# Q projection and O normalisation packed two head groups to a tile, with a new tile table

## The chip, the core and the metric

The kernel runs on one core of one Trainium2 chip. The metric is the device time of one execution in microseconds. Several executions are timed; all that are quoted here are of the state "fast". The span in a profile is some 1.7 to 2.0 us shorter than the time of the same execution. The experiments were made on four chips, each time beside the kernel before, whose median there was 802.84 to 803.36 us; times of different runs are compared across chips with that spread in mind.

## The reference, cut to what matters

```python
B, S, D, H = 1, 2048, 512, 32;  Dh = 16
xn = layernorm(x)
q = (xn @ wq) in 32 heads;  k = xn @ wk;  v = xn @ wv        # one k and v for all heads
p = softmax(q k^T / sqrt(Dh))                                # 32 heads x 2048 x 2048
attn = (p v, heads side by side) @ wo
ffn  = gelu(xn @ w1 + b1) @ w2 + b2                          # F = 1792
return x + attn + ffn
```

The dearest thing is the exponential of 32 x 2048 x 2048 scores. A head has only 16 columns, so everything that is laid out by head fills few of the 128 rows of a tile unless something packs it.

## The kernel before

Queries are cut into 4 blocks of 512 and heads into 8 groups of 4. A score tile is 128 keys x 512 queries of one head; there are 2048 of them, handled in 683 units of three. Each of the four heads of a group sits at its own 32-row strip (16 rows of Q, one row for the softmax shift, 15 of zeros), so that TensorE can work on three tiles at once: near 300 us in the profile before, three score matmuls together take 0.39 us, as long as one.

```python
def scores(u):                       # TensorE: three tiles into three PSUM banks, two sets of banks
    for o, l, rh, q0 in pieces:
        ins = e.matmul(o, l, rh, start=True, stop=True, tile_position=(q0, 0))
def exp(u):                          # ScalarE: the two or three tiles that are not VectorE's
    exps.append(act(lambda e: e.activation(E[:, s0:s0 + na, :], bank(b0, na)..., ACT.Exp, scale=LN2 / 128.0), ...))
    for i, t in enumerate(ts):
        if is_d[t]:
            p1(t, 3 * x + i)         # VectorE: PSUM to int16, then four shifted copies a batch of three
```

A string DTAB has one character a unit and says which tile VectorE takes: "." none, "0" or "2" the first or last. Such a tile costs TensorE five value matmuls (one a shifted copy) in place of one.

Beside this stream run the feed-forward part, the output projection and the Q projection, all as side work in the gaps. Q and O before the change:

```python
def q_proj(tb, hq, bk, ...):         # weights padded to 32 columns a head: 4 heads fill 128 columns
    for d in range(DT):
        (f or mm)(bank(bk), wqp[:, d, 4 * hq:4 * hq + 4, :]..., xnT[:, d, tb * TBW:(tb + 1) * TBW], ...)
def q_evac(tb, hq, bk, **kw):
    dve(lambda e: e.tensor_copy(QT[:, hq, :], bank(bk)), ...)            # cast, one group
    dve(lambda e: e.tensor_tensor(sqq[:, sq(hq), :], QT[:, hq, :], QT[:, hq, :], ALU.mult), ...)
def o_evac(gg):                      # ... reciprocal row sums through DRAM into rbc ...
    onorm[gg] = dve(lambda e: e.tensor_tensor(oT[:, gg % NOT, :], Of[:, i, :], rbc[:, i, :], ALU.mult), ...)
    for j in range(HG):              # then 4 small copies pack 16 rows each
        dma("sp", oTp[r0:r0 + Dh, ...], oT[32 * j:32 * j + Dh, ...], ...)
```

The order in which each engine runs its instructions is fixed when the program is built: a list scheduler (`Prog.schedule`) with estimated durations sorts all operations. Its computed end of the last operation is called **the scheduler's clock** below. It is no measurement.

Of the kernel before, what the change touches and what calls it, by code (L numbers as in the profile page):

```python
# [7 lines left out]
ALU = mybir.AluOpType  # L8
# [30 lines left out]
NE_ND_KB = (24, 8, 3)  # L39
# [11 lines left out]
DTAB = "...00.0020..2.0202....00022022..2002.0.0...000...0.02.02.2220...2022.20222.220.202...200.00.00.20.000.20..20.02.0.22000.02000...202.22.002.0.00.20....220..00022002.2.20...0002.02022.0.2220....222222.22.22020.00...22222.22.00.2.000.0..220...2.0220..0202....22202.020.2.22.222...202..0...2.02200.2...22.0.2..2..00..2000...22.0022.00.2002.02...20220.02.2202.2020...2222.20.202202.2220...2022.200220..0.00....222.0..2022.20.0.20....200.02.20.0..0200....2.220..220.200.02....222.20...02000.200..2.000..0222222.020....2202.22002022..022...2222.02.020222.2.20..222200.0202.222.22.....2..20.2.202.2..0.......0...2202..220.20..2.0..20.0..2.200000...0200.2.2200.00202....22022200..020.2000...."  # L51
# [5 lines left out]
S_LAT = 0.27  # L57
YS = 9
# [367 lines left out]
def bass_parallel_sum__grouped_kv_mqa__dense_activation_gelu__prompt_kernel(  # L426
# [27 lines left out]
    NOT, NPR, NSQ = 3, 5, 4  # L454
# [6 lines left out]
    with ExitStack() as es:  # L461
# [6 lines left out]
        wq_s = ub[:, 8:12, :]  # L468
# [3 lines left out]
        wqp = sb([P, DT, H, 32], bf, "wqp")  # L472
# [19 lines left out]
        sel8 = sb([P, 8, 32], bf, "sel8")  # L492
        selr = sb([P, 4, 32], bf, "selr")
        sel8R = sb([P, 8, 32], bf, "sel8R")
# [21 lines left out]
        hb = sb([P, 6 + NSQ, TBW], bf, "hb")  # L516
# [6 lines left out]
        rbc = sb([P, 2, TBW], f32, "rbc")  # L523
        rX = rbc[:, 1, :].rearrange("p (i r) -> p i r", i=4)
        rd_dram = nc.dram_tensor("rden_rows", [NTB * NGR, HG * TBW], f32).ap()
        oT = sb([P, NOT, TBW], bf, "oT")
# [51 lines left out]
        dma("act", wq_s, A_wq.rearrange("(k p) n -> p k n", p=P), "d_wq", w=[("u", i) for i in range(8, 12)], due=0.0,  # L578
# [22 lines left out]
        dve(lambda e: e.memset(wqp[:, :, :, Dh:32], 0.0), w=["wqp"], n=1024, due=0.1)  # L601
# [4 lines left out]
        sel_diag = bass.AP(sel8[:].tensor, sel8[:].offset, [list(sel8[:].ap[0]), [33, 8], [8, 4]])  # L606
# [6 lines left out]
        for v, c in enumerate((1.0,) + SPL_C):  # L613
            setup(lambda e, v=v, c=c: e.memset(V1[:, v, :, Dh:Dh + 1], c), r=["V1"], w=["V1"], due=11.0)
        setup(lambda e: e.memset(sel8[:], 0.0), w=["sel8"], occ=0.3, due=12.0)
        setup(lambda e: e.tensor_copy(sel_diag, mask4[:].unsqueeze(1).to_broadcast([P, 8, 4])),
              r=["mask4", "sel8"], w=["sel8"], due=12.0)
# [114 lines left out]
        def q_proj(tb, hq, bk, f=None, **kw):  # L732
            for d in range(DT):
                (f or mm)(bank(bk), wqp[:, d, 4 * hq:4 * hq + 4, :].rearrange("p a n -> p (a n)"),
                          xnT[:, d, tb * TBW:(tb + 1) * TBW], d == 0, d == DT - 1,
                          r=["wqp" if hq else "wqp0"] + tr(4 * tb, 4 * tb + 4), w=[B(bk)], **kw)

        def sq(hq):
            return 6 + hq % NSQ

        def q_evac(tb, hq, bk, **kw):
            dve(lambda e: e.tensor_copy(QT[:, hq, :], bank(bk)),  # L742
                w=[B(bk)] + [(B(bk), j) for j in range(4)] + [("QT", hq)] + [("QTm", hq, j) for j in range(4)], **kw)
            dve(lambda e: e.tensor_tensor(sqq[:, sq(hq), :], QT[:, hq, :], QT[:, hq, :], ALU.mult),
                r=[("QT", hq)], w=[("h", sq(hq))], mode=2, **kw)

        def q_first(hq, bk):
            q_proj(0, hq, bk, due=10.5)
            q_evac(0, hq, bk, due=Q_DUE)

        def q_first_m(hq, bk):
            mm(bank(bk), selr[:].rearrange("p a n -> p (a n)"), sqq[:, sq(hq), :], False, True,
               r=["selr", ("h", sq(hq))], w=[B(bk)], skip=True, due=16.0)
            dve(lambda e: e.tensor_scalar(QT[:, hq, :].bitcast(i16), bank(bk).bitcast(i32), isc[:, 0:1], ibi[:, 0:1],
                                          ALU.mult, ALU.add),
                r=["isc", "ibi"], w=[B(bk), ("QT", hq)] + [("QTm", hq, j) for j in range(4)], due=16.0)
# [7 lines left out]
        def wq_first():  # L764
            setup(lambda e: e.tensor_copy(wqp[:, :, 0:4, 0:Dh], wq_s[:, :, 0:64].rearrange("p k (h n) -> p k h n", n=Dh)),
                  r=[("u", i) for i in range(8, 12)] + ["wqp"], w=["wqp0"], occ=0.45, due=9.0)
# [6 lines left out]
        for _, _, kind, a in sorted(steps, key=lambda s: s[:2]):  # L773
            if kind == "ln":
                ln_batch(list(range(*a[:2])), a[2])
            elif kind == "tr":
                x_T(list(range(*a[0])), a[1], a[2])
            elif kind == "k":
                k_proj(list(range(*a[0])), a[1])
            elif kind == "v":  # L780
                v_tiles(range(*a))
                if a[1] in (NVA, NT):
                    k_max(0 if a[1] == NVA else NVA, a[1], land(a[1] - 1) + KM_DUE)
            else:
                wq_first()
                q_first(0, 7)
# [9 lines left out]
        q_first_m(0, 7)  # L796
# [8 lines left out]
        for v, c in enumerate(SPL_C):  # L805
# [3 lines left out]
        setup(lambda e: e.tensor_copy(wqp[:, :, 4:H, 0:Dh], wq_s[:, :, 64:D].rearrange("p k (h n) -> p k h n", n=Dh)),  # L809
              r=[("u", i) for i in range(8, 12)] + ["wqp"], w=["wqp"], occ=2.7, due=19.0, after=[pr.writer["ibi"]])  # L810
# [24 lines left out]
        def scores(u):  # L835
# [3 lines left out]
            for i, t in enumerate(ts):  # L839
# [4 lines left out]
                r += [("KT", kt), ("QT", g), ("QTm", g, j)]  # L844
# [65 lines left out]
        def o_evac(gg):  # L910
# [7 lines left out]
            for j in range(HG):  # L918
                src = rd_dram[gg:gg + 1, j * TBW:(j + 1) * TBW]
                dma("sp", rbc[32 * j:32 * j + 32, i, :], bass.AP(src.tensor, src.offset, [[0, 32], [1, TBW]]),  # L920
                    f"d_rb{i}{j}", r=[("rd", i)], w=[("rbc", i, j)])
            tb, g = divmod(gg, NGR)
            onorm[gg] = dve(lambda e: e.tensor_tensor(oT[:, gg % NOT, :], Of[:, i, :], rbc[:, i, :], ALU.mult),  # L923
                            r=[("Of", i)] + [("rbc", i, j) for j in range(HG)], w=[("oT", gg % NOT)], allow=3.0)
            pp, h = divmod(gg, 2)
            if gg == NTB * NGR - 2:
                setup(lambda e: e.memset(oTp[64:P, pp % NPR, :], 0.0), w=[("oTp", pp % NPR, 1, j) for j in range(HG)], occ=0.4)
            for j in range(HG):
                r0 = 64 * h + Dh * j
                dma("sp", oTp[r0:r0 + Dh, pp % NPR, :], oT[32 * j:32 * j + Dh, gg % NOT, :], f"d_op{gg % NOT}{j}",  # L930
                    r=[("oT", gg % NOT)], w=[("oTp", pp % NPR, h, j)])

        def o_norm_last(gg):
            RB1 = [("rbc", 1, j) for j in range(HG)]
            for h in range(2):
                c = slice(h * 256, h * 256 + 256)
                dve(lambda e, c=c: e.tensor_copy(Of[:, 0, c], pO[:, c]), w=["O", ("Of", 2 * h)], n=256, due=0.0)
            for h in range(2):
                for i in (2 * h, 2 * h + 1):
                    mm(bank(h)[:, 4 * i:4 * i + 4], Of[:, 0, i * P:(i + 1) * P], selL[:], True, True,  # L940
                       r=[("Of", 2 * h), "selL"], w=[B(h)], occ=0.2, due=0.0)
            for h in range(2):
# [5 lines left out]
                if h == 0:  # L948
                    dve(lambda e, o=o, i_=i_: e.tensor_copy(o, i_), r=[("rT", h)], w=[("rX", h)] + RB1, n=256, due=0.0)
                else:  # L950
                    act(lambda e, o=o, i_=i_: e.activation(o, i_, ACT.Copy), r=[("rT", h)], w=[("rX", h)] + RB1, n=256, due=0.0)
# [4 lines left out]
            for h in range(2):  # L956
                c = slice(h * 256, h * 256 + 256)
                dve(lambda e, h=h, c=c: e.tensor_tensor(oT[:, gg % NOT, c], Of[:, 0, c], bank(h)[:, 128:384], ALU.mult),
                    r=[("Of", 2 * h)], w=[B(h), ("oT", gg % NOT) if h == 0 else ("oTl", 1)], n=256, due=0.0)

        def q_group(tb, hqs, rel):
            for hq in hqs:
                q_proj(tb, hq, 7, mm4, allow=QP_ALLOW)
                q_evac(tb, hq, 7, allow=EV_ALLOW)

        def q_m(tb, hqs, **rel):
            pq = tb % 2
            for n, hq in enumerate(hqs):
                mm(pM[0:32, :], sel8R[:, hq, :], sqq[:, sq(hq), :], n == 0, n == len(hqs) - 1, r=["sel8R", ("h", sq(hq))], w=[M4[0]], tp=(0, 0), kind="side", tag=(None, 0))
# [4 lines left out]
            for j in range(4):  # L974
                dst = QT[32 * j + 16:32 * j + 17, h0:h0 + n, :]
                dma("sp", dst, mT[8 * j + h0:8 * j + h0 + n, :], f"d_m{j}",
                    r=["mT"] + [("QT", hq) for hq in hqs], w=[("QTm", hq, j) for hq in hqs])
# [28 lines left out]
        def wo_mm(tb, i, ps, start=False, bk=7, al=1.5):  # L1006
            for n, p in enumerate(ps):
# [4 lines left out]
                   r=[("oTp", pp % NPR, h, j) for h in range(2) for j in range(HG)] + ["wop"], w=[B(bk)], allow=al)  # L1012
# [40 lines left out]
        def q_pair(tb, hqs, u, ms=None):  # L1053
            for i, hq in enumerate(hqs):
                at(u + 1.5 * i, lambda tb=tb, hq=hq: q_group(tb, [hq], {}), 0.93)
            ms = hqs if ms is None else ms
            if ms:
                at(u + 1.5 * len(hqs), lambda tb=tb, ms=ms: q_m(tb, list(ms)), 0.6)
# [151 lines left out]
```

## Time and profile before

| | before |
|---|---|
| time, median of 4 runs | 803.29 us (802.88 to 803.58) |
| span of the profile | 800.7 us |
| busy: TensorE, VectorE, ScalarE | 774.6, 747.7, 780.0 us |
| ScalarE's exponentials, L867 | 683 instructions, 741.4 us |

Three engines are over 90% busy. Such a table cannot say which of them binds. A word on the busy column of ScalarE: neighbouring instructions overlap in the records by some 0.3 us, so idle time shorter than that hides inside "busy".

### The profile page before, as it was taken

Reading aid. Unit: us, or ns where it says so; the run is one execution under the profiler, and the core shown is the slowest. Engines: PE = TensorE matmul, PEld = TensorE weight load, DVE = VectorE, ACT = ScalarE, POOL = GpSimd, SP = SyncE. Lnnn points to the kernel's source line nnn. Section 1 sums busy time; section 2 is a strip of 40 time slices with the busy share of each in tenths; the row PEclk is TensorE's granted clock in tenths of the full one; section 3 lists DMA queues with packets and bytes.
Section 4 is the critical chain, followed back from the end, with each engine's and each line's share of the span. In section 5 each row is a group of like instructions: output and inputs, shape, how many; then the busy total and the mean of one; then the engine's idle time right before and its main releaser. Section 6 shows DMA issues by size and latency. Waiting matters only on the chain.

```text
span 800.7 us, 21071 instructions
## 1 busy us (share of the span) xinstructions
PE 774.6 (97%) x8986; PEld 241.8 (30%) x8986; DVE 747.7 (93%) x1425; ACT 780.0 (97%) x734; POOL 21.9 (3%) x81
## 2 busy tenths in 40 slices
PE   6799999999999999999999999999999999999997
PEld 4323323232232322232232233323333233323222
DVE  7599999999999979999999979999999997899996
ACT  5899999999999999999999999999999999999996
POOL 6400000000000000000000000000000000000000
PEclk9799999999999999999999999999999999999999
DMA  9100000000000100000000000000000001000001
GB/s 311 35 5 18 17 18 19 15 11 19 17 20 22 32 25 7 18 19 18 16 16 15 25 25 25 16 6 19 18 16 19 25 25 33 7 18 16 19 6 44
DMA packets 28023, 21.17 MB, mean 26 GB/s; under 512 B 14369, under 2 KB 23450, under 8 KB 27930
## 3 DMA queue, kind: packets, MB, share of 16 engines
q1 hardware_dynamic: 26346, 19.27, 8.3%
q8 instruction: 71, 1.16, 0.6%
q10 hardware_dynamic: 1584, 0.56, 0.3%
q14 instruction: 22, 0.18, 0.1%
HBM read 15.05 MB, written 2.35 MB: 22 GB/s over the span
## 4 chain that ended last, share of the span: by engine, by line
ACT 81%; PE 11%; DVE 6%; DMA 1%; POOL 1%; issue 0%; ACTq 0%; DVEq 0%
ACT E L867 77%; PE pAll L888 4%; PE pAll L563 3%; PE pAll L848 3%; ACT ub L997 2%; DVE Dt L899 1%; DVE Dt L884 1%; DMA ub<-in_A_wq_dram 1%; DVE hb L983 1%; ACT ub L687 1%; PE pAll L557 1%; DVE ub L999 0%; POOL V L806 0%; DVE ub L994 0%; ACT xnT L705 0%; DVE ub L684 0%
## 5 line engine op out<-in xcount | busy, mean ns | idle before, releaser
L867 ACT ACTIVATE E<-pAll 128x1024 bf16<-128x1024 f32 (+1 forms) x683 | 741.4, 1334 | 1.4 <-PE pAll L848 1.3
L888 PE MATMUL pAll<-Dt,V 128*32 128x512 bf16 x2130 | 370.8, 383 | 0.4
L884 DVE TENSOR_SCALAR Dt<-pAll 128x512 int16<-128x512 f32 x426 | 286.5, 684 | 29.3 <-PE pAll L848 28.5
L888 PE MATMUL pAll<-E,V 128*32 128x512 bf16 x1622 | 298.0, 388 | 0.4 <-DVE Of L912 0.3
L899 DVE TENSOR_SCALAR Dt<-Dt 128x1536 int16<-128x1536 int16 (+2 forms) x600 | 291.5, 529 | 0.7
L848 PE MATMUL pAll<-QT,KT 32*128 32x512 bf16 x2048 | 268.7, 387 | 11.3 <-ACT E L867 5.1
L848 PEld LDWEIGHTS pAll<-QT,KT 32*128 32x128 bf16 x2048 | 68.2, 91 | 289.6 <-ACT E L867 228.2
L888 PEld LDWEIGHTS pAll<-Dt,V 128*32 128x32 bf16 x2130 | 99.2, 94 | 103.3 <-issue 52.3
L563 PE MATMUL pAll<-w_sb,ub 128*32 128x512 bf16 x896 | 122.2, 382 | 0.0
L563 PE MATMUL pAll<-xnT,w_sb 128*32 128x512 bf16 x896 | 111.0, 382 | 0.3
L888 PEld LDWEIGHTS pAll<-E,V 128*32 128x32 bf16 x1622 | 70.8, 94 | 77.6 <-issue 62.2
L563 PE MATMUL pAll<-wop,oTp 128*32 128x512 bf16 x256 | 48.7, 381 | 0.1
L983 DVE TENSOR_SCALAR hb<-pAll,b1T 128x512 bf16<-128x512 f32 x56 | 41.7, 745 | 2.0 <-PE pAll L563 1.8
L563 PE MATMUL pAll<-xnT,wqp 128*32 128x512 bf16 x496 | 39.4, 390 | 0.4 <-POOL wqp L809 0.3
L563 PEld LDWEIGHTS pAll<-w_sb,ub 128*32 128x32 bf16 x896 | 33.2, 95 | 13.2 <-issue 5.2
L1171 PE MATMUL pAll<-xnT,zeros 128*32 128x512 bf16 x332 | 36.8, 384 | 0.0
L563 PEld LDWEIGHTS pAll<-xnT,w_sb 128*32 128x32 bf16 x896 | 29.6, 95 | 20.2 <-issue 8.6
L997 ACT ACTIVATE ub<-ub 128x1536 bf16<-128x1536 bf16 (+1 forms) x20 | 30.9, 1543 | 0.0
L742 DVE CAST QT<-pAll 128x512 bf16<-128x512 f32 x32 | 21.8, 682 | 3.0 <-PE pAll L563 2.9
L912 DVE COPY Of<-pAll 128x512 f32<-128x512 f32 x31 | 21.1, 682 | 0.1
L923 DVE TENSOR_TENSOR oT<-Of,rbc 128x512 bf16<-128x512 f32 x31 | 21.2, 684 | 0.0
L999 DVE TENSOR_TENSOR ub<-ub,hb 128x1536 bf16<-128x1536 bf16 (+1 forms) x20 | 18.0, 899 | 0.1
(119 smaller groups left out, 270.3 us busy)
## 6 DMA issues: line engine op xcount, KB each, us to landing
rbc<-rden_rows SPq DMA_DIRECT2D x124, 64.0 KB, 2.0
w_sb<-in_B_w_dram SPq DMA_DIRECT2D x2, 1792.0 KB, 13.0
x_sb<-in_A_x_dram SPq DMA_DIRECT2D x8, 256.0 KB, 6.9
out_dram<-x_sb SPq DMA_DIRECT2D x16, 128.0 KB, 1.8
oTp<-oT SPq DMA_DIRECT2D x124, 16.0 KB, 1.8
ub<-in_A_wq_dram ACTq DMA_DIRECT2D x1, 512.0 KB, 7.7
wop<-in_A_wo_dram SPq DMA_DIRECT2D x1, 512.0 KB, 16.7
den<-Of SPq DMA_DIRECT2D x31, 8.0 KB
```

The source lines that it names most:

```text
L563: add("pe", lambda e, c=c, j=j: e.matmul(o[c, :], l[:, c], rh, start=start, stop=stop, tile_position=(0, 32 * j)), r, [(k, j) for k in w] ...
L742: dve(lambda e: e.tensor_copy(QT[:, hq, :], bank(bk)), w=[B(bk)] + [(B(bk), j) for j in range(4)] + [("QT", hq)] + [("QTm", hq, j) for j i ...
L848: ins = e.matmul(o, l, rh, start=True, stop=True, tile_position=(q0, 0))
L867: exps.append(act(lambda e: e.activation(E[:, s0:s0 + na, :], bank(b0, na).rearrange("p (a n) -> p a n", a=na), ACT.Exp, scale=LN2 / 128.0 ...
L884: dve(lambda e: e.tensor_scalar(Dt[:, KZ, s, :], bank(bk), float(127 * 128) + SPL_D, SPL_MIN, ALU.add, ALU.max), w=[B(bk), ("D", s, KZ)], ...
L888: add("pe", lambda e, a, b: e.matmul(pO[32 * j:32 * j + 32, :], V1[:, v, kt, :], rhs, start=a, stop=b, tile_position=(0, 32 * j)), r=r + [ ...
L899: dve(lambda e, k=k: e.tensor_scalar(Dt[:, k, s0:s0 + n, :], Dt[:, KZ, s0:s0 + n, :], float(SPL_K[k]), None, ALU.add), r=[("D", s0 + i, KZ ...
L912: dve(lambda e: e.tensor_copy(Of[:, i, :], pO), w=["O", ("Of", i)], allow=0.0)
L923: onorm[gg] = dve(lambda e: e.tensor_tensor(oT[:, gg % NOT, :], Of[:, i, :], rbc[:, i, :], ALU.mult), r=[("Of", i)] + [("rbc", i, j) for j ...
L983: dve(lambda e: e.tensor_scalar(hb[:, ft % 6, :], pM, b1T[:, ft:ft + 1], None, ALU.add), r=["b1T"], w=M4 + [("h", ft % 6)], allow=ev)
L997: act(lambda e: e.activation(uu, uu, ACT.Tanh, scale=GELU_K), r=uk, w=uk, n=c, allow=al - 0.5, kind="tanh")
L1171: pr.filler = lambda e, j, o: e.matmul((pO if o else pM)[32 * j:32 * j + 32, :], zeros[:, 0:32], xnT[:, 0, 0:TBW], start=not o, stop=not o ...
```

## The change

The intent is to halve VectorE's and TensorE's side work for Q and O by working on 128 full rows (two groups of 64 useful rows), to move rows between the packed and the padded layout by DMA, and to spend what this frees on more tiles for VectorE. The string DTAB is replaced whole: 439 tiles for VectorE where there were 426. E, the buffer of exponentials, gets 25 slots for 24, and a parameter Q3 places the last Q pack of a block.

```diff
-NE_ND_KB = (24, 8, 3)
+NE_ND_KB = (25, 8, 3)
-DTAB = "...00.0020..2.0202....00022022.. (683 characters, 426 of them 0 or 2)
+DTAB = "...00.20.0022.00.2...202202.22.. (683 characters, 439 of them 0 or 2)
+        def q_pack(tb, p, gls=(0, 1)):
+            for d in range(DT):
+                mm4(pM, wq_sb[:, d, P * p:P * (p + 1)], xnT[:, d, tb * TBW:(tb + 1) * TBW], ...)
+            dve(lambda e: e.tensor_copy(qp[:, s, :], pM), ...)
+            dve(lambda e: e.tensor_tensor(sqq[:, 6 + s, :], qp[:, s, :], qp[:, s, :], ALU.mult), ...)
+            for gl in gls:
+                for j in range(HG):
+                    dma("sp", QT[32 * j:32 * j + Dh, 2 * p + gl, :], qp[r0:r0 + Dh, s, :], ...)
 ... o_evac:
-            onorm[gg] = dve(... oT[:, gg % NOT, :], Of[:, i, :], rbc[:, i, :], ALU.mult ...)
-                dma("sp", oTp[r0:r0 + Dh, pp % NPR, :], oT[32 * j:32 * j + Dh, gg % NOT, :], ...)
+                dma("sp", OfP[r0:r0 + Dh, s, :], Of[32 * j:32 * j + Dh, i, :], ...)
+                dma("sp", rbP[r0:r0 + Dh, s, :], <reciprocal row, repeated 16 times>, ...)
+            if h or end:
+                onorm[gg - h] = onorm[gg] = dve(... oTp[0:n, sl, :], OfP[0:n, s, :], rbP[0:n, s, :], ALU.mult ...)
 ... (cut: allocations, the zeroing of QT, selector masks, call sites, the tail's buffers)
```

## The prediction

> **What bounds the kernel now.** The work is 2048 score tiles (4 query blocks, 8 head groups, 64 tiles a group) in 683 units of three. TensorE makes three tiles at a time in PSUM, ScalarE turns two or three of them into exponentials in one instruction, and a table gives at most one tile of a unit to VectorE, which makes it as a sum of five shifted approximations. I read the page first: busy times, then the slices, then the chain of work that ended last.
>
> ```profile
> PE 774.6 (97%) x8986; PEld 241.8 (30%) x8986; DVE 747.7 (93%) x1425; ACT 780.0 (97%) x734; POOL 21.9 (3%) x81
> ACT  5899999999999999999999999999999999999996
> ACT 81%; PE 11%; DVE 6%; DMA 1%; POOL 1%; issue 0%; ACTq 0%; DVEq 0%
> ```
>
> Three engines look full, so busy shares decide nothing. The chain is 81% ScalarE. TensorE's share also holds the 332 matmuls against zeros that only keep its clock up. The waits tell the engines apart:
>
> ```profile
> PEld pAll L848 <- ACT E L867: 228.2, 539, 2.0
> PEld pAll L848 <- DVE Dt L884: 25.8, 57, 0.9
> DVE Dt L884 <- PE pAll L848: 28.5, 36, 4.7
> ACT E L867 <- PE pAll L848: 1.3, 3, 0.7
> ```
>
> (waiter, what it waited for: us in total, times, longest). TensorE's score matmuls wait 228 us for ScalarE to free PSUM; ScalarE waits 1.3 us for anything in its whole exponential stream. The view of stretches says the same by query block (sum of the four steady stretches: ScalarE busy 744.95 of 745 us):
>
> ```profile
> 40.00:210.00 170.00, 166.71 (x1853) 50.48 (x1849) 168.69 (x322) 170.00 (x160) 0.00 (x0) 1.00 0.06 16
> 210.00:403.00 193.00, 190.36 (x2187) 56.79 (x2187) 182.33 (x343) 193.00 (x179) 0.00 (x0) 1.00 0.07 19
> 403.00:596.00 193.00, 191.35 (x2254) 58.88 (x2251) 185.50 (x356) 193.00 (x180) 0.00 (x0) 1.00 0.07 19
> 596.00:785.00 189.00, 186.47 (x2316) 56.55 (x2313) 176.05 (x327) 188.95 (x174) 0.52 (x1) 1.00 0.07 19
> ```
>
> (columns after the length: TensorE, weight load, VectorE, ScalarE, GpSimd, clock, DMA share, GB/s). VectorE is at 99% in the first block and 93 to 96% later. So ScalarE sets the time from the first exponential, at 29.45 us, to the last, near 792 us; before it stands a prologue and after it a tail of 8.7 us that is one dependent chain. What matters next is the price of one tile on ScalarE, which the grouped durations give only roughly, because neighbours overlap; the timeline of ScalarE in narrow windows gives starts (start, length, what):
>
> ```profile
> 586.41 2.15 ACT L867 ACTIVATE E<-pAll 128x1024 bf16<-128x1024 f32 x2
> 587.31 2.17 ACT L867 ACTIVATE E<-pAll 128x1024 bf16<-128x1024 f32 x2
> 588.22 2.18 ACT L867 ACTIVATE E<-pAll 128x1024 bf16<-128x1024 f32 x2
> 590.02 1.72 ACT L867 ACTIVATE E<-pAll 128x1536 bf16<-128x1536 f32 x1
> 591.35 1.30 ACT L867 ACTIVATE E<-pAll 128x1024 bf16<-128x1024 f32 x1
> ```
>
> Each row shows the first start. Two-tile exponentials start 0.905 us apart (586.41, 587.31, 588.22), the three-tile one is followed after 1.33 us (590.02 to 591.35). A tile costs ScalarE 0.425 us.
>
> **What the Trainium skill says.** "ScalarE: Activation LUTs", section "What ACT_TABLE_LOAD costs", gives 0.833 ns per element and an overlap of about 93 ns of neighbours. 512 elements are then 0.427 us: the trace agrees on the slope, though the overlap it shows is larger (a two-tile instruction lasts 1178 ns in the mean and starts recur every 905). "VectorE: DVE Perf Modes", section "The perf-mode tier table", lets one-source operations on 16-bit data in SBUF run at four elements a cycle, two-source ones at two, fp32 two-source and fp32 PSUM reads at one. The trace agrees: 551 ns for 1536 elements (L899), 412 ns for a bf16 square of 512 (L744), 684 ns for 512 fp32 (L884, L923). So VectorE's cost follows columns, not filled rows, and packing two groups of 64 useful rows into one tile halves it. The same page, section "Zero memsets can be issued as uint32", counts one cycle per element; the memset of 1024 took 912 ns. "DMA: Bandwidth & Descriptors", section "Rules for kernel authors", advises to issue early and wait late, because the fixed cost then overlaps; here a small SBUF copy landed 1.8 us after issue.
>
> **The change, part by part.** Rows used:
>
> ```profile
> L884 DVE TENSOR_SCALAR Dt<-pAll 128x512 int16<-128x512 f32 x426 | 286.5, 684 | 29.3 <-PE pAll L848 28.5
> L742 DVE CAST QT<-pAll 128x512 bf16<-128x512 f32 x32 | 21.8, 682 | 3.0 <-PE pAll L563 2.9
> L923 DVE TENSOR_TENSOR oT<-Of,rbc 128x512 bf16<-128x512 f32 x31 | 21.2, 684 | 0.0
> L744 DVE TENSOR_TENSOR hb<-QT 128x512 bf16<-128x512 bf16 x32 | 13.2, 412 | 0.0
> oTp<-oT SPq DMA_DIRECT2D x124, 16.0 KB, 1.8
> ```
>
> *Q.* One padded group at the start and 16 packs in place of 32 groups: 15 casts at 0.682 and 15 squares at 0.412 go, 16.4 us of VectorE. One of ten bit-trick evacuations goes (0.67). On TensorE 496 column-tiled matmuls become 256; 16 of them take 1.05 us in the timeline, so 240 are 15.8 us. Added: 8 small copies a pack, 124 in all, on the DMA queue.
> *O.* 31 normalising multiplies become 15 for pairs and one for the last lone group: 15 at 0.684, 10.3 us of VectorE. The copies into packed rows stay 124 in number but now precede the multiply.
> *Table.* Counted in the diff: 439 tiles go to VectorE where 426 did. Each costs VectorE one L884 and its share of the shifts (291.5/426 = 0.684), with L884 at 286.5/426 = 0.673: 1.357 us, so 13 are 17.6 us. TensorE runs five value matmuls for such a tile in place of one: 52 more at some 0.06 us, 3 us.
> *Sums.* VectorE: -16.4 - 0.7 - 10.3 + 17.6 = -9.8 us. TensorE about -12.7. ScalarE: 13 tiles at 0.427, -5.55 us. Only the last lies on the path. By block, the added tiles are 3, 4, 4 and 2, and VectorE's savings exceed them everywhere: in the first, tight, block 6 of 13 cast-and-square pairs go (6.6), some 3 multiplies (2.1) and one evacuation, for 4.1 us added.
> *Ends.* A memset of Q's tile, 2048 words, is an estimated 1.8 us (double the 0.91), less 0.64 for the shorter weight memset; VectorE has 1.55 us idle there before the first input lands, so it is hidden. The 1.68 us weight copy on GpSimd (L809), for which the first Q projection waited at 31.9, goes; ScalarE's two idle spots just after it (0.49 and 0.18 us before 35.06 and 38.52) should shrink. I book -0.3. The tail's chain is unchanged.
> *Result.* 803.34 - 5.55 - 0.3 = 797.5 us. I chose to grant nothing for a larger buffer of exponentials (25 slots for 24): a wait of ScalarE on it doesn't show.
>
> **Rivals.** *The whole saving shows:* if VectorE's or TensorE's work were the bound, the 27.4 us removed before the refill would give some 776. For it: VectorE's 99% in the first block. Against it: the refill spends 17.6 of it, and ScalarE has no idle time to give. *VectorE turns into the bound:* denser tiles of its own reach ScalarE as late frees of PSUM; score matmuls already wait 25.8 us on L884. If a fifth of the 439 tiles delayed ScalarE by 0.1 us, 9 us, the time would be 806. Against it: VectorE's load falls in every block and it waits 28.5 us itself. *A DMA takes the place of the copy:* Q now reaches its rows 2 us after the cast, behind a queue that waits in order, and VectorE's multiply waits for 16 copies. If every pack stalled scores for 2 us, 32 us, 835. Against it: after the first block every pack is placed some 124 units, about 135 us, before its first use. In the first block the first pack follows exponential 0; four copies at 0.59 us issue each, the mask chain and two landings put it near 42 us (an estimate), and unit 21 needs it near 53. The queue's issue time rises from an estimated 177 to 248 us of 800, still a third.
>
> **Range and chances.** ScalarE's saving is countable, its spread the 0.418 to 0.427 us a tile, 0.1 us in all. The rest is how well the new table keeps ScalarE fed: small late frees could return up to 2.5 us, and the prologue could give 1 to 2. Hence 795.5 to 800.0, lopsided for stalls. Two per cent is 16 us: three times what ScalarE can gain, and a loss of that size needs the DMA rival nearly in full. Faster 0.01, same 0.97, slower 0.02.
>
> **What would show it.** Right: exponentials of 128x1024 number 440 and of 128x1536 number 243 (13 over), start intervals unchanged, ScalarE still busy all but 0.1 us of the steady stretches, VectorE near 738 us, TensorE's wait for ScalarE above 200 us. Wrong: ScalarE idle on score matmuls that wait on Q's rows (DMA) or on L884, idle time before the paired multiply, or a first exponential later than 29.5 us. Any of these over 3 us in sum breaks the range.

## The result, and the profile after

| | before | after |
|---|---|---|
| time, median of 4 runs | 803.29 us | 797.95 us (797.41 to 798.72) |
| span of the profile | 800.7 us | 795.8 us |
| busy: TensorE, VectorE, ScalarE | 774.6, 747.7, 780.0 us | 767.0, 739.8, 774.0 us |
| exponentials, two tiles / three tiles | 427 / 256 | 440 / 243 |

The ratio is 0.9935, with a 95% interval from 0.9917 to 0.9952. Ratios here are the mean time of one kernel's fast runs over that of the other's of the same rounds, so they are not quite the ratio of the medians quoted. The interval leaves out 1. The time lies 0.45 us above the prediction, inside its range.

The lines of the changed kernel that answer to those of the prediction, first from the page (busy times and the chain), then the waits (waiter, what it waited for: us, times, longest), then the stretches (TensorE, weight load, VectorE, ScalarE, GpSimd, clock, DMA share, GB/s):

```profile
PE 767.0 (96%) x8759; PEld 240.5 (30%) x8759; DVE 739.8 (93%) x1401; ACT 774.0 (97%) x734; POOL 20.8 (3%) x84
ACT 92%; PE 5%; DVE 3%; DMA 0%; issue 0%; DVEq 0%
```

```profile
PEld pAll L851 <- ACT E L870: 222.9, 525, 1.9
PEld pAll L851 <- DVE Dt L887: 29.2, 64, 0.9
DVE Dt L887 <- PE pAll L851: 28.3, 33, 4.3
```

```profile
40.00:210.00 170.00, 165.19 (x1757) 49.96 (x1753) 166.62 (x318) 169.95 (x161) 0.00 (x0) 1.00 0.08 18
210.00:403.00 193.00, 190.30 (x2185) 57.51 (x2183) 179.81 (x340) 193.00 (x181) 0.00 (x0) 1.00 0.08 19
403.00:596.00 193.00, 189.89 (x2194) 57.89 (x2191) 184.22 (x345) 192.40 (x180) 0.00 (x0) 1.00 0.08 19
596.00:785.00 189.00, 186.27 (x2295) 56.58 (x2296) 178.18 (x330) 189.00 (x176) 0.88 (x1) 1.00 0.08 17
```

The picture is the same as before with a shorter stream: ScalarE is busy in all but 0.65 us of the 745, VectorE is a little lighter in the first three stretches, and TensorE waits about as long as before for ScalarE. (In the last stretch the shorter program has come further, so its VectorE does more in it.) The groups by shape show the packed operations (x count, busy us and mean ns, idle before):

```profile
L973 DVE CAST qp<-pAll 128x512 bf16<-128x512 f32 x16 | 10.9, 682 | 0.4 <-PE pAll L567 0.4
L937 DVE TENSOR_TENSOR oTp<-OfP,rbP 128x512 bf16<-128x512 f32 x15 | 10.2, 682 | 0.1
L974 DVE TENSOR_TENSOR hb<-qp 128x512 bf16<-128x512 bf16 x16 | 6.6, 412 | 0.0
```

They last as long as the unpacked ones did and are half as many. The paired multiply, which now waits for sixteen copies, stood idle 0.1 us in total for them.

Where did the time go? The span splits at the first and the last exponential. ScalarE's timeline in narrow windows, the first two rows from the kernel before, then two from the changed one:

```profile
29.45 1.45 ACT L867 ACTIVATE E<-pAll 128x1536 bf16<-128x1536 f32 x1 [0.66 <-PE pAll L848]
790.94 1.10 ACT L867 ACTIVATE E<-pAll 128x1024 bf16<-128x1024 f32 x1
```

```profile
30.00 1.45 ACT L870 ACTIVATE E<-pAll 128x1536 bf16<-128x1536 f32 x1 [0.66 <-PE pAll L851]
785.36 1.28 ACT L870 ACTIVATE E<-pAll 128x1024 bf16<-128x1024 f32 x1
```

The same two of the second profile of the changed kernel, which comes from the run "after_again" below:

```profile
28.76 1.45 ACT L870 ACTIVATE E<-pAll 128x1536 bf16<-128x1536 f32 x1 [0.61 <-PE pAll L851]
784.70 1.26 ACT L870 ACTIVATE E<-pAll 128x1024 bf16<-128x1024 f32 x1
```

| part of the span, us | before | after | after, second profile | change (to second) |
|---|---|---|---|---|
| to the first exponential | 29.45 | 30.00 | 28.76 | +0.55 (-0.69) |
| start of the first to start of the last | 761.49 | 755.36 | 755.94 | -6.13 (-5.55) |
| from there to the end | 9.8 | 10.4 | 10.4 | +0.6 (+0.6) |

In the second profile the stream got shorter by 5.55 us, which is what 13 tiles at 0.427 us cost; in the first by 6.13 us. The program is the same, so these parts are known to about 0.6 us. Prologue and tail moved by about as much.

The starts in the packed traces say whether a tile's price changed. The median time from the start of one exponential to the start of the next is 904 ns for two tiles and 1330 ns for three, before and after. What all such intervals (with nothing else of ScalarE between) take beyond that is called **late starts** below. They sum to 10.0 us before, and to 9.5 and 10.1 us in the two profiles after. This catches small waits of ScalarE that the overlap of the records hides, and it didn't change: the gain is the count of tiles.

### The profile page after: what moved, and what is told of

Read it like the earlier page. It is cut to its first block, busy times and chain, and to the rows that moved or that the text cites. A ratio compares the mean times of both kernels' runs of the same rounds, so it can differ in the third digit from the quotient of the medians.

```text
span 795.8 us, 20778 instructions
## 1 busy us (share of the span) xinstructions
PE 767.0 (96%) x8759; PEld 240.5 (30%) x8759; DVE 739.8 (93%) x1401; ACT 774.0 (97%) x734; POOL 20.8 (3%) x84
## 4 chain that ended last, share of the span: by engine, by line
ACT 92%; PE 5%; DVE 3%; DMA 0%; issue 0%; DVEq 0%
ACT E L870 88%; ACT ub L1012 3%; PE pAll L891 2%; PE pAll L851 1%; DVE stats L660 1%; PE pAll L567 1%; PE pAll L561 1%; DVE Dt L887 0%; DVE Dt L902 0%; DMA x_sb<-in_A_x_dram 0%; ACT xnT L718 0%; PE pAll L713 0%; ACT KT L732 0%; ACT ub L700 0%; DVE ub L697 0%
## 5 line engine op out<-in xcount | busy, mean ns | idle before, releaser
L891 PE MATMUL pAll<-Dt,V 128*32 128x512 bf16 x2195 | 390.0, 383 | 0.3
L887 DVE TENSOR_SCALAR Dt<-pAll 128x512 int16<-128x512 f32 x439 | 292.9, 680 | 28.9 <-PE pAll L851 28.3
L891 PE MATMUL pAll<-E,V 128*32 128x512 bf16 x1609 | 303.2, 387 | 1.4 <-DVE Of L915 1.2
L902 DVE TENSOR_SCALAR Dt<-Dt 128x1536 int16<-128x1536 int16 (+1 forms) x608 | 297.6, 533 | 0.9
L851 PEld LDWEIGHTS pAll<-QT,KT 32*128 32x128 bf16 x2048 | 68.8, 91 | 290.4 <-ACT E L870 222.9
L891 PEld LDWEIGHTS pAll<-Dt,V 128*32 128x32 bf16 x2195 | 105.6, 94 | 107.0 <-issue 54.8
L567 PE MATMUL pAll<-xnT,w_sb 128*32 128x512 bf16 x896 | 128.1, 382 | 0.1
L567 PE MATMUL pAll<-xnT,wq_sb 128*32 128x512 bf16 x256 | 20.5, 398 | 0.0
L1011 DVE TENSOR_TENSOR ub<-ub,hb 128x1536 bf16<-128x1536 bf16 (+1 forms) x20 | 17.9, 893 | 0.1
L1014 DVE TENSOR_TENSOR ub<-ub,hb 128x1536 bf16<-128x1536 bf16 (+1 forms) x20 | 17.9, 894 | 0.1
L1009 DVE TENSOR_TENSOR ub<-hb 128x1536 bf16<-128x1536 bf16 (+1 forms) x20 | 17.8, 892 | 0.1
```

Of the source, the lines that this page charges most:

```text
L567: add("pe", lambda e, c=c, j=j: e.matmul(o[c, :], l[:, c], rh, start=start, stop=stop, tile_position=(0, 32 * j)), r, [(k, j) for k in w] ...
L887: dve(lambda e: e.tensor_scalar(Dt[:, KZ, s, :], bank(bk), float(127 * 128) + SPL_D, SPL_MIN, ALU.add, ALU.max), w=[B(bk), ("D", s, KZ)], ...
L891: add("pe", lambda e, a, b: e.matmul(pO[32 * j:32 * j + 32, :], V1[:, v, kt, :], rhs, start=a, stop=b, tile_position=(0, 32 * j)), r=r + [ ...
L902: dve(lambda e, k=k: e.tensor_scalar(Dt[:, k, s0:s0 + n, :], Dt[:, KZ, s0:s0 + n, :], float(SPL_K[k]), None, ALU.add), r=[("D", s0 + i, KZ ...
L1011: dve(lambda e: e.tensor_tensor(uu, uu, hh, ALU.mult), r=uk + hk, w=uk, n=c, mode=2, allow=al)
L1014: dve(lambda e: e.tensor_tensor(uu, uu, hh, ALU.mult), r=uk + hk, w=uk, n=c, mode=2, allow=al)
```

## The experiments

Three questions were open. Is the gain the count of tiles on ScalarE, as predicted? Is the packing needed for it, or had the other engines room anyway? And what moves the prologue?

**1. The unaltered change, again.** No edit.

> The changed kernel unaltered, as the partner of the other runs on the same chip. Both theories: some 5 to 6 us under the kernel before (797 to 798.5 us), first exponential within 0.6 us of 30.0 us in the span. If the half-clock stretch of TensorE near 8 to 18 us in the prologue is a matter of chance it is absent in this profile; if it comes from the program it is there again.

Measured: 798.01 us median of 5 (796.85 to 799.06), ratio 0.9934 (0.9922 to 0.9946). The five runs fall in two groups by granted clock: 796.85 and 796.99 us at 0.994, and 798.01, 798.75 and 799.06 us at 0.989. The stretch from 8 to 18 us in the view of stretches (TensorE busy, clock, DMA share, GB/s) shows the difference; the three rows are of the kernel before, the changed kernel's first profile, and this one:

```profile
8.00:18.00 10.00, 6.21 (x62) 1.00 1.06 381
```

```profile
8.00:18.00 10.00, 7.54 (x49) 0.50 1.07 374
```

```profile
8.00:18.00 10.00, 6.95 (x65) 1.00 1.07 377
```

In the first profile of the changed kernel TensorE ran at half clock here; in this one it did not, and the first exponential started 1.24 us earlier (28.76 for 30.00). The program is the same, so the stretch comes and goes from execution to execution. It is not the changed kernel's own either: of the 14 profiles kept, only this one and that of the kernel before have 1.00 here. The other twelve, of both programs and their variants, have 0.50 to 0.83. Compared without it on both sides, the spans are 800.7 and 795.1 us: 5.6 us apart.

**2. The packing with the old table, and the new table without the packing.**

```diff
 (pack_oldtab: the changed kernel)       (nopack_newtab: the kernel before)
-DTAB = <439 tiles>                      -DTAB = <426 tiles>
+DTAB = <426 tiles, of before>           +DTAB = <439 tiles, of after>
```

> The change with the tile table of before (426 tiles on VectorE). Theory A (only the count of tiles on ScalarE matters; packing by itself is off the path): 803.3 us within 1 us of the kernel before. Theory B (a table and the static order computed from it fit only the program they were searched for, so that a foreign table costs stalls whatever its count): the scheduler's own clock, which was 5.6 us under the profile's span for both kernels, gives 803.3 for this one in place of 795.0, so near 811 us, with ScalarE idle some 8 us more before its exponentials. Rival C (VectorE's and TensorE's savings show by themselves): under 800 us.

> The kernel before with the new table (439 tiles on VectorE) and nothing else. If the table alone made the gain: 797.8 us. Theory A: 13 tiles off ScalarE (-5.5 us) but 17.6 us more on VectorE, which was at 99 per cent of the first block: 798 to 806 us. Theory B: the scheduler's clock says 833.6, so near 841 us, with ScalarE waiting 30 us or more for scores that wait for VectorE.

Measured: 809.77 us (ratio 1.0081, 1.0067 to 1.0095) and 840.32 us (1.0463, 1.0448 to 1.0477). Theory B's numbers, 811 and 841, hold to about 1 us. Its idle time for the packed program with the old table holds in part only: it said some 8 us more before the exponentials, and the late starts grew by 4.5 us (14.5 for 10.0), while the last operation of ScalarE waited 5.4 us in place of 2.2 in the tail. Neither half of the change gains anything by itself, and the new table on the old program loses 37 us. In that profile ScalarE waits for scores:

```profile
ACT E L867 <- PE pAll L848: 31.6, 22, 13.3
```

The kernel before has 1.3 us in this place. But this pair doesn't yet tell what the packing is worth: both tables were searched for another program, and a foreign table costs stalls of its own. A fair test must either leave the order untouched or search a table anew for each program. The next runs do the former, the last two the latter.

**3. VectorE's saving given back, order untouched.** Each packed cast, square and multiply runs through its columns twice, the second time into a spare slot.

```diff
-dve(lambda e: e.tensor_copy(qp[:, s, :], pM), ...)
+dve(lambda e: e.tensor_copy(spare(qp, s, 2), tw(pM)), ...)      # out and in: 2 x 512 columns
 (the same for the square into hb and the multiply into oTp)
```

> The changed kernel with its static order untouched, in which each packed cast, square and multiply works through its 512 columns twice (the second pass goes to a spare slot): 16 times 0.53 + 0.27 + 0.53 us give VectorE some 21 us of the 27 us back that the packing removed. The result stays correct. Theory A (the packing pays for the 13 tiles by making room on VectorE): VectorE has no room for both, ScalarE waits for late frees of PSUM, 803 to 812 us against 798.0 for the changed kernel. Rival E (VectorE had room anyway and the packing was not needed): within 1.5 us of 798.0.

Measured: 812.37 us, ratio 1.0116 (1.0103 to 1.0129), result correct: 14.4 us above the changed kernel. The three operations lengthened to 1215, 679 and 1215 ns, so 16 x (0.533 + 0.267 + 0.533) = 21.3 us were added (an estimate from these durations), and two thirds of it showed. The page's chain and two waits of this run:

```profile
PE 44%; DVE 39%; ACT 13%; issue 2%; DMA 1%; DVEq 1%; ACTq 0%; POOL 0%
```

```profile
PEld pAll L851 <- ACT E L870: 176.7, 431, 1.7
PEld pAll L851 <- DVE Dt L887: 36.5, 77, 1.2
```

ScalarE's share of the chain fell from 92% to 13%. Its late starts sum to 25.1 us, 15 more than in the changed kernel, and that is the time lost. Rival E falls: VectorE had no such room.

**4. TensorE's saving given back, order untouched.** Two tries, each with 256 matmuls against zeros. In the first they stand as blocks of 16 before each pack, in the second one after each matmul of the pack.

```diff
+for k in range(16):                            # tensor_again: ahead of the pack's first matmul
+    e.matmul(pM[32*j:32*j+32, :], zeros[:, 0:32], xnT[:, 0, 0:TBW], start=True, stop=True, ...)
+f(e); e.matmul(pM[32*j:32*j+32, :], zeros[:, 0:32], ..., start=False, stop=True, ...)   # tensor_spread
```

> The changed kernel with its static order untouched and 16 matmuls against zeros ahead of each of the 16 packed projections, 256 in all, some 0.85 us a pack: TensorE gets its 13.7 us back. Correct result. Theory A (TensorE's saving is off the path, it waits over 220 us for ScalarE): 798 to 800 us. Rival F (TensorE's saving pays as much as VectorE's): 805 us or more.

> The changed kernel, order untouched; after each of the 16 matmuls of a packed projection one more against zeros in the same column group, accumulating, so 256 in all as in the run before it, but spread over the places where the projection's matmuls stand and not in one block ahead of them. Result correct. If TensorE's saving is off the path (theory A) and the 11 us of the blocked run came from one block of 0.85 us delaying the next scores: 798 to 801 us. If TensorE has no room for them wherever they stand (rival F): 805 us or more.

Measured: 808.85 us for the block (1.0067, 1.0054 to 1.0080), with a wrong result that was not meant: the scheduler may put matmuls of the other column groups ahead of the pack's first, and the block then clears their sums. Building this run's program again supports that: in one of the 16 packs, the second of the first query block, three matmuls of other column groups stand ahead of the first. That this alone made the error was not tested. The spread version is correct and took 808.06 us (1.0059, 1.0044 to 1.0074), 10.1 us above the changed kernel for an estimated 13.7 us of work (256 of some 53 ns; in the trace of the first try, the pack's matmuls start 0.87 us after a block of 16 does, so 54 ns each). Page of the spread run:

```profile
PE 42%; ACT 41%; DVE 15%; issue 1%; DMA 1%; DVEq 0%; ACTq 0%; POOL 0%
```

ScalarE's late starts are 20.6 us in both tries, 10.5 to 11.1 more than in the changed kernel, which again is the time lost. So the block was not the main reason: the two differ by 0.8 us. Theory A's 798 to 800 falls and rival F holds: TensorE had no room either, although its score matmuls still waited 205.0 us for ScalarE in this run.

**5. The kernel before with VectorE relieved, order and table untouched.** Its output is wrong, which doesn't matter for the time.

```diff
+cw = TBW if tb == 0 else 64                    # multiplies: TBW if gg < NOT else 64
-dve(lambda e: e.tensor_copy(QT[:, hq, :], bank(bk)), ...)
+dve(lambda e: e.tensor_copy(QT[:, hq, 0:cw], bank(bk)[:, 0:cw]), ...)
 (the same for the square and the multiply)
```

> The kernel before with its static order and its own table untouched; casts and squares of Q work on 64 of 512 columns from the second query block on, multiplies on 64 from the fourth group on, so the result is wrong on purpose. VectorE is spared some 24 x 0.70 + 28 x 0.47 = 30 us, as much as the packing spares it. Theory A (packing alone is off the path): within 1 us of the kernel before, 803.1. Rival C (VectorE's saving shows by itself): 795 us or less.

Measured: 802.65 us, ratio 0.9992 (0.9980 to 1.0004). Twenty-four casts shrank to 219 ns, as many squares to 179 and 28 multiplies to 215 ns. VectorE's busy time fell from 747.7 to 724.6 us, and its wait for scores grew from 28.5 to 44.5 us:

```profile
DVE Dt L885 <- PE pAll L849: 44.5, 72, 4.7
```

Of the 23.1 us freed, 16.0 turned into this wait, and ScalarE's late starts stayed at 9.9 us. A lighter VectorE alone is worth nothing, as predicted. The counterpart, the kernel before with TensorE alone relieved in its own order, was not run.

**6. ScalarE thinned in both kernels, order untouched.** 480 of 512 columns once a buffer slot has been filled. Their outputs are wrong, which doesn't matter for the times.

```diff
+cw = TBW - 32 if all(s0 + k in efull for k in range(na)) else TBW
-e.activation(E[:, s0:s0 + na, :], bank(b0, na)..., ACT.Exp, ...)
+e.activation(E[:, s0:s0 + na, 0:cw], bank(b0, na)...[:, :, 0:cw], ACT.Exp, ...)
```

> The kernel before, order untouched, with every exponential after the first turn of its buffer working on 480 of 512 columns (wrong on purpose): some 1600 tiles at 27 ns, 43 us less of ScalarE. Shows how far the next bound is. If ScalarE alone binds and the others have wide room: 770 us or less. If the three engines are balanced, as the busy shares suggest: 790 to 800 us.

> The same thinning on the changed kernel. Where the packing has made more room than the 13 tiles use up (VectorE 739.8 us busy against 747.7), the thinned changed kernel lies further below its own time than the thinned kernel before does below its own: 780 to 792 us. If the new table has used up all the room, the fall is no larger than before's.

Measured: 794.82 us (0.9890, 0.9875 to 0.9905) and 790.31 us (0.9835, 0.9819 to 0.9851). Some 42 us, an estimate, were taken from ScalarE (32 columns at 0.83 ns, the slope of the start intervals, in about 1600 tiles) and 8.5 us came off the kernel before, 7.7 us off the changed one. What the score matmuls waited for in the thinned changed kernel:

```profile
PEld pAll L851 <- ACT E L873: 107.1, 256, 1.7
PEld pAll L851 <- issue: 105.8, 311, 0.6
PEld pAll L851 <- DVE Dt L891: 41.4, 96, 1.1
```

"Issue" is time in which the profile shows nothing to wait for. It was 19.3 us in the changed kernel. The 222.9 us of waiting for ScalarE shrank by more than half, yet the time fell by only 1%. The chains of the two thinned kernels, before and after:

```profile
PE 70%; DVE 26%; ACT 1%; issue 1%; DMA 1%; POOL 1%; DVEq 0%; ACTq 0%
PE 62%; DVE 30%; ACT 4%; issue 2%; DMA 1%; DVEq 0%; ACTq 0%; POOL 0%
```

The next bound, TensorE with VectorE, lies right behind ScalarE in both kernels. The new table has used up the room that the packing made: the changed kernel does not fall further than the kernel before. It still ends 4.5 us ahead of it, so the packing moved that next bound by about as much as the table moved ScalarE.

**7. More matmuls against zeros at the start**, against the half-clock stretch.

```diff
-pr.pro_filler = lambda e: e.matmul(bank(3)[:, 0:256], zeros[:], zr, start=True, stop=True, ...)
+pr.pro_filler = lambda e: [e.matmul(bank(3)[:, 0:256], zeros[:], zr, ...) for _ in range(2)][1]
```

> The changed kernel with each of the 23 matmuls against zeros at the start issued twice, so that TensorE's pause between about 6 and 10 us shrinks. If the half-clock stretch near 8 to 18 us that some executions of the changed kernel have (granted clock 0.989 in place of 0.994) comes from that pause and costs the first exponential 1.2 us, it is gone in every run: all runs near 797.0 us, median about 1 us under 798.0. If it is chance of another kind: the same two groups of times as the changed kernel, 797 and 798 to 799 us. If the added matmuls delay the transposes: a first exponential later than 30.0 us.

Measured: 797.94 us (0.9932, 0.9920 to 0.9945), runs from 796.48 to 799.42 us: two of the six near 797, the rest higher, and the profile again has TensorE below full clock between 8 and 18 us (0.83 in the mean). The pause did shrink, to 1.39 us in this profile, and from 14 to 16 us the clock was 0.50 all the same. The stretch is not removed by shortening the pause. What sets it is left open.

**8. A table searched anew for each program.** A random search over tables, about 3600 trials each against the program's own scheduler, from one scrambled 439-tile table; only the string differs from the kernel before and the changed one.

> The kernel before with a table found by a random search against the program's own scheduler, the same search, effort and scrambled 439-tile starting table as in the next run. The scheduler's clock gives 805.7 for it (411 tiles); the profile's span was 4 to 6 us above that clock for the other tables and the time 1.7 to 2.6 us above the span, so 812 us within 2. If the packing gives the room that a table can use (theory A), this one is slower than the next run by about the 8.5 us between the two clocks. If the packing is worth nothing under equal search (rival E): within 2 us of the next run.

> The packed kernel with a table from the same search and start. The scheduler's clock gives 797.1 (424 tiles on VectorE, two fewer than the kernel before's own table): 804 us within 2. Theory A: about 8.5 us faster than the run before this one, and no faster than the kernel before's own well-searched table. Rival E: within 2 us of the run before this one.

Measured: 814.75 us with 411 tiles (1.0144, 1.0125 to 1.0164) and 805.14 us with 424 (1.0023, 1.0005 to 1.0041). My search is weaker than the one behind the tables of the two kernels, for both stay slower than the kernel before. But under equal search the packed program is 9.6 us faster and carries 13 tiles more. It is one search for each from one start, so how much is the luck of the search is not known. With only Q or only O packed the same search ended at scheduler's clocks of 802.7 and 801.8 us, between 805.7 (nothing packed) and 797.1 (both). These two were not run on the chip.

The scheduler's clock against the chip, over six tables:

| program and table | scheduler's clock, us | time, us |
|---|---|---|
| before | 795.0 | 803.3 |
| after | 790.3 | 798.0 |
| packed, table of before | 803.3 | 809.8 |
| not packed, table of after | 833.6 | 840.3 |
| not packed, searched | 805.7 | 814.8 |
| packed, searched | 797.1 | 805.1 |

The difference is 6.5 to 9.1 us throughout. This also bears on a part of the change that no run took away, the 25th slot, which every packed program here has and no unpacked one. Built again with 24 slots, the changed kernel keeps its scheduler's clock of 790.3 us; the kernel before with 25 keeps its 795.0; and no exponential waited for a slot in the profile of either. So it is unlikely to matter, but the chip was not asked. Q3 was not varied on the chip either.

No run gave a version clearly faster than the changed kernel that also computes the right result.

## Why the prediction was right or wrong

**The number was right, and so was its main term.** The prediction booked 13 tiles at 0.427 us, 5.55 us, for ScalarE. The exponentials are 440 and 243 as foreseen, their start intervals are unchanged, and the stream shrank by 5.55 us in one profile and by 6.13 in the other. That the first figure agrees to two decimals is luck. One of the prediction's signs failed: ScalarE was to be busy in all but 0.1 us of the steady stretches and missed 0.65, of which 0.6 is a single wait for scores in the third. That stayed far below the 3 us at which the prediction gave up its range.

**"Only the last lies on the path" holds for a saving and fails for a load.** A VectorE lighter by 23 us of busy time moved the kernel before by less than 0.1%: right. For TensorE the saving alone was not tested. What the prediction left out is that the new table needs TensorE's saving as well as VectorE's. It set the added tiles against VectorE's savings only, block by block, and booked TensorE's 12.7 us as worth nothing. Giving 13.7 us of work back to TensorE cost 10.1 us of time, although its score matmuls waited 205 us for ScalarE; and taking 42 us from ScalarE freed only 8. My reading is that the wait stands at a fixed place in a fixed order, where a score matmul waits for its bank, and later matmuls cannot fill it; the total of the wait says where the time is spent, not how much room there is. In this order the three engines are balanced to within about 8 us. The 12.7 us themselves were too large: the prediction priced a Q matmul from 16 that take 1.05 us to the end of the last, and from start to next start 16 take 0.87 us, so 240 of them are some 13.0 us and not 15.8. TensorE's busy time fell by 7.6 us, with 24 matmuls against zeros fewer as well.

**The refill needed the packing.** The prediction counted VectorE's net load as -9.8 us; its busy time fell 7.9. It said that the savings exceed the added tiles in every block, and the rival "VectorE turns into the bound" did not come true in the change itself. The run that gives VectorE its work back shows how near it was: 812 us. The two searched tables point the same way by another road, 9.6 us.

**The rival of the full saving** (776 us) fell in the change; in the relieved kernel before only its half on VectorE was tried, and fell. **The rival of the DMA** fell too: no score matmul waited for a copy of Q, and the paired multiply stood idle 0.1 us in total. What the prediction took from the Trainium skill, "DMA: Bandwidth & Descriptors", section "Rules for kernel authors", to issue early and wait late, held in these rows: a copy of Q took 1.8 us (median) from issue to landing.

**The ends: one within the scatter, one mis-sized.** The prologue was booked at -0.3. It is -0.69 without the half-clock stretch and +0.55 with it; the prediction did not know that stretch and counted a first exponential after 29.5 us as a sign against itself. The other profiles show how much chance is in this. At a mean clock of 0.66 from 8 to 18 us the first exponential starts at 29.34 and 29.32 us in the order of the kernel before ("before_light", "thin_before") and at 29.06, 29.21 and 29.54 us in that of the changed one ("vector_again", "tensor_spread", "thin_after"). So -0.3 is neither shown nor refuted. The memset was hidden as worked out: it lasted 1.765 us and VectorE then still waited 0.57 us for input. "The tail's chain is unchanged" is true of its instructions, but it grew by 0.6 us. From the first copy of the last group's sums to the transposes of its reciprocals it takes 2.02 us before (792.56 to 794.58) and 2.47 us after (786.48 to 788.95 in the second profile). Half of that comes before the sums reach TensorE: it starts on them 0.48 us after the copy begins before and 0.73 us after, with six projection matmuls placed there. The other half comes just before the transposes, again with projection matmuls that the new order put there; rows of the kernel before, then of the second profile of the changed one:

```profile
794.04 0.61 PE L563 MATMUL pAll<-wop,oTp 128*32 128x512 bf16 x8
794.58 0.44 PE L954 MATMUL pAll<-ident_f,rbc 128*128 128x128 f32 x2
```

```profile
788.19 0.83 PE L567 MATMUL pAll<-wop,oTp 128*32 128x512 bf16 x9
788.95 0.44 PE L961 MATMUL pAll<-ident_f,rbP 128*128 128x128 f32 x2
```

This is read from the trace; no run took those matmuls away. In the first profile the ends cost 1.15 us where -0.3 was booked, and the stream gave 0.58 us more than booked; in the second profile the ends come to -0.09 us. That the median lies only 0.45 us from 797.5 is therefore in part luck.

## What to carry to other kernels

When several engines are over 90% busy, test for room by loading one engine without changing the order: here a wait of some 220 us on TensorE was no room, and only a run showed it. A saving on an engine that isn't last in the chain can be worth nothing until work is moved onto it from the engine that is, as VectorE's was here. A table or order searched for one program must be searched again before a part of a change is judged alone.

## What the Trainium skill lacked or had wrong

- "Perfetto Trace Analysis", section "Identifying the Most-Contended Engine", takes the occupancy of ScalarE and VectorE as a fair measure and says to optimise the engine with the highest first. Here ScalarE was busy in 744.95 of 745 us, and taking an estimated 42 us from it gave 8.5 us. The page has no test for engines that bind together.
- "ScalarE: Activation LUTs", section "What ACT_TABLE_LOAD costs", gives 186 ns + 0.833 ns an element with immediate scale and bias, and about 93 ns of overlap between neighbours, so some 93 ns fixed in a stream. The exponentials of 1024 elements start 0.905 us apart, which leaves 0.05 us beside 0.853; they last 1178 ns in the mean, so neighbours overlap by some 0.27 us.
- "TensorE: Matmul & The Clock Gate", section "Why this matters for your kernels", names an idle gap above about 3 us as what brings the half clock back. The kernel before paused 4.30 us in its prologue and kept full clock from 8 to 18 us; the changed kernel paused 4.26 us and lost it in one profile, 3.41 us and kept it in another. With the pause cut to 1.39 us part of the stretch still ran at half clock (0.83 in the mean). So the length of the gap alone did not decide it in these runs.
- No page has what an order fixed at build time does to slack: an estimated 21.3 us added to VectorE cost 14.4 us, an estimated 13.7 us added to TensorE cost 10.1, and 23 us taken from VectorE gave nothing.
